# Grouping the half-height matmuls of a feed-forward block by four pairs, and spreading the side work of an attention loop over its tiles

## Chip, cores and metric

One core of a Trainium2 chip. The metric is the device time of one execution in microseconds (us), with the median of several executions as the time of a kernel. A profile is one execution of a kernel; its span is about 1.7 us shorter than the device time of the same execution.

## The reference

A transformer block whose LayerNorms are modulated by a vector `c`: linear attention with 32 heads of 18 channels, then a ReLU feed-forward part. All data are bfloat16; there are S = 2048 tokens, D = 576 and Dff = 4608.

```python
mod = (_silu(c) @ w_mod).reshape(1, 6, 1, -1)        # sa, ca, ga, sb, cb, gb
h = _layernorm(x) * (1 + ca) + sa
q, k, v = split(h @ wqkv)                            # 32 heads x 18
pq, pk = q @ w_phi, k @ w_phi                        # per head, 18 x 18
phi_q = concat([softmax(pq), softmax(-pq)])          # over the 18 channels
phi_k = concat([softmax(pk), softmax(-pk)])
kv, z = phi_k^T @ v, sum_s phi_k                     # no S x S matrix
o = (phi_q @ kv) / (phi_q @ z + 1e-6)
x = x + ga * (o @ wo)
h = _layernorm(x) * (1 + cb) + sb
x = x + gb * (relu(h @ w1) @ w2)
```

## The kernel before

The kernel first folds `w_phi` into the weights of k. A loop over 16 tiles of 128 tokens then does k, v, the softmax of k, and the accumulation of `kv` in PSUM. Other work is laid between the tiles: the fold of `w_phi` into the weights of q (five transposed weight blocks, then five fold steps), the transposed LayerNorm output ("features") for the next four tiles, the q projections, and rows and columns of the modulation. Then come two tiles of attention output, and the feed-forward part in five blocks of 2, 4, 4, 4 and 2 tiles, with the attention output of the next block's tiles inside.

Inside `manual_schedule` an engine's instructions keep the order of the program text. In the loop a scheduler orders them; `issue_after(x)` keeps an instruction behind `x`. `two()` gives one of two pairs of PSUM banks, `one()` a single bank.

```python
def k_tile(t):                                       # v_tile(t) is alike
    ps = two()
    project(lambda bk: ps[:, bk, :], lambda ci: hT[:, ci, t*P:(t+1)*P], wk_sb, HALF)   # 10 matmuls
    E = E_sb[:, t % NE]                              # NE = 3
    for sgn in range(2):
        nc.scalar.activation(out=E[:, sgn, :]..., in_=ps[:, :, 0:HD2], func=ACT.Exp, scale=1.0 - 2.0*sgn)

def k_softmax(t):
    nc.vector.tensor_reduce(out=R[:, 0, :], in_=E, axis=AXX, op=ALU.add)
    ...                                              # reciprocal
    for sgn, eng in ((1, nc.gpsimd), (0, nc.vector)):
        eng.tensor_tensor(out=e, in0=e, in1=..., op=ALU.mult)

def kv_tile(t):
    for g, (h0, nh) in enumerate(GRP):               # 5 groups of heads
        for sgn in range(2):
            nc.tensor.matmul(kvacc[g // 2][...], lhsT=E_sb[:, t % NE, sgn, ...], rhs=v_sb[:, t % NV, g, ...], ...)

for t in range(NT + 1):
    if t < NT:
        k_tile(t)
        v_tile(t)
        u = t + 4
        if u < NT:
            with tc.issue_after(held):               # held: LayerNorm of tile 3, so long past
                ln_stats(0, u)
            if u % 2:
                ln_rstd(0, u - 1, u + 1); ln_apply(0, u - 1); ln_apply(0, u)
            if u % 4 == 3:
                to_features(u - 3, 4, one, hT, (u - 3)*P, mod1, "aavva", 0)
    if 1 <= t <= NT:
        k_softmax(t - 1)
    if 2 <= t <= NT:
        kv_tile(t - 2)
    if t < NT:
        if t + 4 < NT and t % 4 == 3:
            for n in (1, 2):
                to_features(t + 1, 4, one, hT, (t + 1)*P, mod1, "aavva", n)
        a_filler(t)       # t=0: all wq transposes; t=1: whole wq fold; t=3: row; t=6: columns; q parts
```

```python
# feed-forward, hidden layer of one block: 18 pairs of hidden tiles
for j in range(NJ // 2):
    pace(9 * nn / 2400)                              # may put attention work here
    hps = [psf(), psf()]
    for half in (0, 1) if j % 2 == 0 else (1, 0):    # so two pairs share one trip to half height
        for n, jj in enumerate((j, j + NJ // 2)):
            # half 0: 4 matmuls over 128 rows; half 1: one matmul over 64 rows, pair members
            # on rows 0-63 and 64-127
            ...
    ...                                              # ReLU
```

The softmax here doesn't subtract the row's maximum and nothing guards it: scores larger than these inputs give would overflow.

## Time and profile before

The kernel before takes 461.5 us (median of four first executions).

| stretch of the profile | us |
|---|---|
| start to the first k tile | 18.5 |
| first k tile to the end of the last kv tile | 92.3 |
| from there to the first feed-forward matmul | 19.8 |
| feed-forward part | 327.7 |

The end of the last kv tile is counted here and below to the start of its last matmul. A granted clock of 0.50 is called half clock. In the views, `two` and `one` are the PSUM banks of the loop, `kvacc` the sums of `kv` in PSUM and `kvzd` their copies, `psf`, `num` and `pt` the PSUM banks of the feed-forward part, `rEQ` the exponentials of q; `rW`, `rV` and `rH` are regions of SBUF that hold weights, v, and the features, exponentials of k and hidden layer.

The stretches follow one another on TensorE, so that what one loses or gains moves all later ones.

### The profile page before, as it was taken

To read this page: it belongs to the slowest core of one execution; us is meant where nothing else is said; L and a number is where in the kernel's file an instruction comes from. 1 tells how busy PE (TensorE), PEld (TensorE's weight loads), DVE (VectorE), ACT (ScalarE), POOL (GpSimd) and SP (SyncE) were. 2 spreads that over 40 slices of the span, in tenths; PEclk is the share of its full clock that TensorE was granted. 3 is DMA by queue.
4 is the path that set the end of the run, shared out by engine and by line. 5 is a ranking of instruction groups with operands and counts; after the bars stand their busy time and mean duration, and the time that the engine had idled before them with its cause. 6 is when DMAs were issued, how large, how long until landed. Compare 5 with 4: busy or idle time off the path is not lost.

```text
span 458.2 us, 8190 instructions
## 1 busy us (share of the span) xinstructions
PE 433.4 (95%) x3448; PEld 297.0 (65%) x3460; DVE 237.5 (52%) x566; ACT 158.6 (35%) x387; POOL 57.8 (13%) x71
## 2 busy tenths in 40 slices
PE   5978999997889999999999999999999999999996
PEld 4756776775567785335888633488863348887775
DVE  4697864564844664334566433555743331564421
ACT  3656676765666412332111232212122230012300
POOL 8022141432111110001111000111100000110000
PEclk9698999999999999999999999999999999999999
DMA  7970750000076000000000000000000000000000
GB/s 230 346 215 0 276 191 2 1 0 3 0 256 210 1 14 14 1 0 1 14 14 14 14 0 1 1 2 26 14 13 1 0 1 13 15 14 14 1 0 28
DMA packets 17151, 22.52 MB, mean 49 GB/s; under 512 B 2010, under 2 KB 16474, under 8 KB 16602
## 3 DMA queue, kind: packets, MB, share of 16 engines
q1 hardware_dynamic: 15904, 21.97, 14.4%
q8 instruction: 27, 0.44, 0.4%
q10 hardware_dynamic: 1210, 0.02, 0.2%
q14 instruction: 10, 0.08, 0.1%
HBM read 19.63 MB, written 2.36 MB: 48 GB/s over the span
## 4 chain that ended last, share of the span: by engine, by line
PE 83%; ACT 6%; DVE 5%; POOL 4%; issue 1%; POOLq 0%; DVEq 0%; ACTq 0%
PE psf L657 31%; PE psf L638 28%; PE two L313 5%; PE psf L643 5%; PE psf L313 4%; PE two L380 2%; POOL rH L346 2%; ACT rH L324 2%; DVE R_sb L338 2%; PE num L518 2%; ACT rEQ L388 1%; PE kvacc L355 1%; POOL rW L164 1%; PE psf L293 1%; PE pt L574 1%
## 5 line engine op out<-in xcount | busy, mean ns | idle before, releaser
L638 PE MATMUL psf<-h2T,rW 128*128 128x512 bf16 (+1 forms) x708 | 132.3, 336 | 1.8 <-issue 0.9
L657 PEld LDWEIGHTS <-rH 128*128 128x128 bf16 x1152 | 111.2, 98 | 27.4
L657 PE MATMUL psf<-rW,rH 128*128 128x288 bf16 x864 | 116.3, 286 | 0.0
L638 PEld LDWEIGHTS <-rW 128*128 128x128 bf16 x720 | 66.5, 98 | 62.2 <-issue 15.3
L647 ACT ACTIVATE rH<-psf 128x256 bf16<-128x256 f32 (+1 forms) x108 | 51.8, 490 | 105.1 <-PE psf L643 84.8
L649 DVE TENSOR_SCALAR rH<-psf 128x512 bf16<-128x512 f32 (+1 forms) x72 | 45.0, 625 | 79.0 <-PE psf L643 39.7
L563 POOL TENSOR_TENSOR o_sb<-rV 128x576 bf16<-128x576 f32 x15 | 21.1, 1408 | 271.7 <-DVE rV L559 271.7
L313 PE MATMUL two<-rW,rH 128*128 128x288 bf16 (+2 forms) x320 | 46.6, 295 | 2.1 <-ACT rH L301 0.8
L657 PE MATMUL psf<-rEQ,rH 128*128 128x288 bf16 x288 | 41.3, 286 | 0.0
L313 PEld LDWEIGHTS <-rH 128*128 128x128 bf16 x320 | 31.5, 101 | 12.4 <-ACT rH L301 1.6
L660 DVE TENSOR_TENSOR yt<-psf,gb_row 128x288 f32<-128x288 f32 x32 | 14.4, 449 | 42.6 <-PE psf L657 42.6
L346 POOL TENSOR_TENSOR rH<-rH,R_sb 128x576 bf16<-128x576 bf16 x16 | 25.7, 1608 | 69.0 <-DVE R_sb L343 28.7
L338 DVE TENSOR_REDUCE R_sb<-rH 128x64 f32<-128x1152 bf16 x16 | 21.6, 1351 | 21.4 <-ACT rH L324 21.3
L272 ACT ACTIVATE rs<-mv,eps_t 128x1 f32<-128x1 f32 (+2 forms) x24 | 7.2, 298 | 58.6 <-DVE mv L269 56.1
L268 DVE BATCH_NORM_STATS2 st<-x_sb 128x6 f32<-128x288 bf16 x60 | 24.7, 439 | 2.0 <-DMA x_sb<-in_A_x_dram 1.6
L643 PE MATMUL psf<-h2T,rW 64*128 64x512 bf16 (+1 forms) x180 | 23.8, 339 | 0.0
L324 ACT ACTIVATE rH<-two 128x576 bf16<-128x576 f32 x32 | 19.3, 663 | 9.0 <-PE two L313 8.0
L546 DVE TENSOR_TENSOR ab<-dz 128x70 f32<-128x70 f32 x16 | 3.7, 232 | 35.4 <-ACT dz L537 35.4
L388 ACT ACTIVATE rEQ<-two 126x512 bf16<-126x512 f32 (+1 forms) x32 | 16.6, 601 | 10.5 <-PE two L380 10.5
L579 ACT ACTIVATE oT<-pt 128x640 bf16<-128x640 bf16 x14 | 9.9, 707 | 29.6 <-PE pt L574 29.6
L313 PE MATMUL psf<-wo_sb,oT 128*128 128x288 bf16 x140 | 19.4, 286 | 0.0
L380 PE MATMUL two<-rH 128*126 128x512 bf16 (+1 forms) x80 | 18.8, 380 | 0.4
(118 smaller groups left out, 389.9 us busy)
## 6 DMA issues: line engine op xcount, KB each, us to landing
rW<-in_B_w_dram SPq DMA_DIRECT2D x1, 4608.0 KB
rW<-in_B_w_dram SPq DMA_DIRECT2D x3, 1296.0 KB, 9.8
rW<-in_w_mod_dram SPq DMA_DIRECT2D x6, 576.0 KB, 7.4
out_dram<-x_sb SPq DMA_DIRECT2D x16, 144.0 KB, 1.8
rEQ<-in_B_w_dram SPq DMA_DIRECT2D x1, 1296.0 KB, 7.4
rW<-in_A_wqkv_dram SPq DMA_DIRECT2D x2, 576.0 KB, 8.8
x_sb<-in_A_x_dram SPq DMA_DIRECT2D x1, 1152.0 KB, 11.8
rW<-in_A_wqkv_dram SPq DMA_DIRECT2D x4, 144.0 KB, 3.1
```

What stands on the lines that cost most here:

```text
L268: nc.vector.bn_stats(out=s[:, hf, :], in_=x_sb[:, t, hf * HD2:(hf + 1) * HD2])
L313: nc.tensor.matmul(ps(bk)[:, 0:cn], lhsT=lhs(ci), rhs=rhs[:, ci, c0:c0 + cn], start=(first and ci == 0), stop=(ci == NC - 1))
L324: nc.scalar.activation(out=E[:, sgn, :].rearrange("p (b f) -> p b f", b=2), in_=ps[:, :, 0:HD2], func=ACT.Exp, scale=1.0 - 2.0 * sgn)
L338: nc.vector.tensor_reduce(out=R[:, 0, :], in_=E, axis=AXX, op=ALU.add)
L346: eng.tensor_tensor(out=e, in0=e, in1=R[:, 1, sgn * H:(sgn + 1) * H].unsqueeze(2).to_broadcast([P, H, DH]), op=ALU.mult)
L380: nc.tensor.matmul(pss[k][0:nf, :], lhsT=wq_sb[:, ci, f0:f0 + nf], rhs=hT[:, ci, sl], start=(ci == 0), stop=(ci == NC - 1))
L388: nc.scalar.activation(out=Eq[b][0:nf, g, sgn, :], in_=pss[k][0:nf, :], func=ACT.Exp, scale=1.0 - 2.0 * sgn)
L638: nc.tensor.matmul(hps[n][:, 0:nn], lhsT=w1a[:, ci, jj * P:(jj + 1) * P], rhs=h2T[:, ci, 0:nn], start=(not last and ci == 0), stop=(last a ...
L643: nc.tensor.matmul(hps[n][:, 0:nn], lhsT=w1b[b0:b0 + 64, j * P:(j + 1) * P], rhs=h2T[b0:b0 + 64, 4, 0:nn], start=not last, stop=last)
L647: nc.scalar.activation(out=H1[:, jj, 0:nn], in_=hps[n][:, 0:nn], func=ACT.Relu)
L649: nc.vector.tensor_relu(H1[:, jj, 0:nn], hps[n][:, 0:nn])
L657: nc.tensor.matmul(ps[:, 0:cn], lhsT=H1[:, j, tt * P:(tt + 1) * P], rhs=w2q[j // 9][:, j % 9, c0:c0 + cn], start=(j == 0), stop=(j == NJ - 1))
```

## The change

The intent is to keep TensorE busy. In the feed-forward part a group is four pairs instead of two, so that fewer trips into half height and back are needed; the PSUM pools of this part then hold 4 + 3 + 1 banks, and four pairs use all of them. In the loop, `kv_tile` runs three tiles behind k instead of two, the side work is spread over the tiles, and it stands ahead of `kv_tile`. At the end of attention, 24 dummy matmuls stand where TensorE waits. The core of the diff (cut: declarations, PSUM handles as lists of single banks, dummy allocations):

```diff
-    NE = 3
+    NE = 4                                   # and NV = 4
     def kv_tile(t):
-        for g, (h0, nh) in enumerate(GRP):
+        for g in (4, 0, 1, 2, 3):            # kv_final in the same order
...
-    def a_filler(t):
+    def filler_1(t):
         if t == 0:
-            fold_transposes(wq_raw, wqT, "av")
+            wq_transposes((0, 1), q_two)     # copies out of PSUM all on ScalarE
+        if t == 1:
+            wq_transposes((4,), lambda n: [one()])
+    def filler_2(t):
+        if t in (3, 7, 11):
+            next_features(t, 2)
+        if t == 0:
+            wq_transposes((2, 3), q_two)
-        if t == 1:
-            fold(wqT, wq_sb, "av")
+        if t in (2, 3):
+            fold(wqT, wq_sb, "av", (2 * t - 4, 2 * t - 3))
-        if t == 3:
-            mod_row(2, ga_row, one)
+        if t == 4:
+            fold(wqT, wq_sb, "a", (4,))
+            row_e(row_mm(2, q_two), ga_row)
...
+    LN_AT = {0: (4, 5), 1: (6, 7)}           # LayerNorm two tiles earlier
+    for t in range(2, NT - 6):
+        LN_AT[t] = (t + 6,)
+    LAG = 3
-    for t in range(NT + 1):
+    for t in range(NT + 2):
         if t < NT:
             k_tile(t)
+            filler_1(t)
             v_tile(t)
-            ...                              # LayerNorm, first part of the features
+        for u in LN_AT.get(t, ()):
+            later(ln_stats, 0, u)            # later: issue_after(held)
+            ...
         if 1 <= t <= NT:
-            k_softmax(t - 1)
+            held = k_softmax(t - 1)          # its reduction
-        if 2 <= t <= NT:
-            kv_tile(t - 2)
         if t < NT:
-            if t + 4 < NT and t % 4 == 3:
-                for n in (1, 2):
-                    to_features(t + 1, 4, one, hT, (t + 1) * P, mod1, "aavva", n)
-            a_filler(t)
+            filler_2(t)
+        if LAG <= t < NT + LAG - 1:
+            kv_tile(t - LAG)
+        if t < 12 and t % 4 in (1, 2):
+            next_features(t, t % 4 - 1)
...
+        size = 2 if b == 0 else 4
+        for j0 in range(0, NJ // 2, size):
+            js = list(range(j0, min(j0 + size, NJ // 2)))
+            for j in first half of js:   full(j, hp[j], False)
+            for j in js:                 rest(j, hp[j], ...)      # the half-height matmuls
+            for j in second half of js:  full(j, hp[j], True); relu(j, hp[j])
...
-    rps = row_mm(5, lambda: num3()[:, 0, :])
+    rps = row_mm(5, q_n3)
+    for _ in range(24):
+        nc.tensor.matmul(spare[0][:, 0:P], lhsT=ident[:, :], rhs=ident[:, :], start=True, stop=True)
```

(The three lines `for j in ...` of the feed-forward part are shortened here.)

## The prediction

> **What bounds the kernel now.** I read the page first (engine shares, then the 40 slices), then cut the span into five stretches with the windows view, then the list of waits of TensorE, then the timeline around the idle places. The slices say where to look:
>
> ```profile
> PE 433.4 (95%) x3448; PEld 297.0 (65%) x3460; DVE 237.5 (52%) x566; ACT 158.6 (35%) x387; POOL 57.8 (13%) x71
> ...
> PE   5978999997889999999999999999999999999996
> ...
> PEclk9698999999999999999999999999999999999999
> ```
>
> TensorE is the bound. It is full from about 130 us to the end (the feed-forward part) and has holes before (the attention part); PEclk is the granted clock. The windows view with the program's own borders (start, first k tile, first q part, last kv tile, first feed-forward matmul, end) sizes this; columns are the stretch, its length, then busy us (instructions) of PE, PEld, DVE, ACT, POOL, then clock and DMA:
>
> ```profile
> 19.77:50.05 30.28, 25.12 (x254) 18.95 (x253) 26.63 (x69) 18.69 (x53) 5.92 (x4) 0.94 0.42 125
> 50.05:110.22 60.17, 56.42 (x471) 41.79 (x471) 35.79 (x47) 40.70 (x86) 19.80 (x12) 1.00 0.23 87
> 110.22:130.45 20.23, 14.87 (x114) 10.25 (x114) 14.32 (x45) 11.55 (x33) 1.40 (x1) 0.92 0.06 11
> 130.45:458.17 327.72, 322.75 (x2450) 213.42 (x2461) 150.16 (x372) 78.89 (x200) 19.72 (x14) 1.00 0.07 24
> ```
>
> So TensorE idles 5.2 us in the second stretch, where VectorE is 88% busy, 3.7 us in the third, 5.4 us in the fourth, and hardly at all in the feed-forward part. Who it waits for (us in total, times, longest), and the two places where a wait is followed by a slow clock (timeline; start, duration, group, idle before it; and two windows):
>
> ```profile
> PE kvacc L355 <- POOL rH L346: 3.3, 5, 0.8
> PE n L518 <- DVE kvzd L367: 1.8, 1, 1.8
> PE two L257 <- ACT rV L333: 1.1, 1, 1.1
> PE kvacc L355 <- DVE rH L346: 0.9, 2, 0.5
> ```
>
> ```profile
> 33.48 6.73 PE L313 MATMUL two<-rW,rH 128*128 128x288 bf16 x40
> ...
> 112.70 2.31 PE L518 MATMUL n<-kvzd,rEQ 126*128 126x140 bf16 x20 [1.80 <-DVE kvzd L367]
> 114.81 5.22 PE L380 MATMUL s<-rH 128*126 128x512 bf16 x20
> ```
>
> ```profile
> 30.42:33.83 3.41, 1.78 (x19) 1.26 (x18) 3.29 (x10) 1.57 (x5) 1.74 (x1) 1.00 0.07 21
> 33.83:37.24 3.41, 3.41 (x17) 2.23 (x15) 1.64 (x6) 1.38 (x3) 0.00 (x0) 0.50 0.00 0
> 108.92:112.34 3.42, 1.16 (x11) 0.70 (x10) 1.92 (x10) 2.07 (x4) 1.25 (x1) 1.00 0.01 2
> 112.34:115.75 3.41, 3.05 (x23) 2.66 (x24) 1.42 (x8) 0.81 (x6) 0.00 (x0) 0.50 0.00 0
> ```
>
> Two stretches of 3.41 us in which TensorE is busy half the time or less are each followed by 3.41 us at half clock. The last view is the feed-forward inner loop: 16 full-height matmuls, then 4 of half height (64 rows, the last 64 of the 576 inputs):
>
> ```profile
> 182.97 0.61 PE L643 MATMUL psf<-h2T,rW 64*128 64x512 bf16 x4
> 183.51 3.63 PE L638 MATMUL psf<-h2T,rW 128*128 128x512 bf16 x16
> 187.07 0.60 PE L643 MATMUL psf<-h2T,rW 64*128 64x512 bf16 x4
> ```
>
> **What the Trainium skill says.** (1) "TensorE: Matmul & The Clock Gate", Part 1 (The HAM clock gate): the clock halves after about one idle window of 3.4 us and comes back after a busy one. The trace agrees on the length (3.41 us) and shows that half-idle is enough: the two windows above are 52% and 34% busy; one of 60% busy at 40.7 us did not trip it. (2) Same page, Part 3 (Packing small matmuls — row/col tiling): matmuls on different row groups run concurrently. The trace agrees: the four half-height matmuls take 0.54 us from first start to the next full one, not four times 0.216. (3) "TensorEngine Tiling (Array Packing)", Tiling Modes, Key Properties: "Mode switching requires drain". The trace agrees: one round is 187.07 - 182.97 = 4.10 us, while 16 full matmuls and 2 pairs at the streaming interval of 0.216 us (16 in 3.63 us, less the modelled 0.38 of the last, over 15 steps) would be 3.89. So one trip into half height and back costs 0.21 us. Single records say the same: 312 ns from the last full start to the first half-height start, 308 ns back, 229 ns from pair to pair; the weight load of 93 ns, hidden elsewhere, stands open at each switch. At 256 columns the excess is the same 0.21 us.
>
> **The change, part by part.** The order of instructions of both kernels, without times, is used below.
>
> *Feed-forward.* Blocks 1 to 4 go over hidden tiles by four pairs instead of two: 2 full pairs, 8 half-height matmuls, 2 full pairs. 18 pairs then need 5 trips instead of 9. A trip saved gives 0.20 us, less the 0.013 us that a further pair-to-pair step costs: 0.184 us. 4 trips x 4 blocks x 0.184 = 2.9 us. Block 0 keeps trips of two pairs, but two of its trips were cut in half by attention work placed inside (205 + 211 ns at such a cut instead of none): the new placement puts that work between, about 0.2 us each. Sum: **3.3 us**, all on the bound engine. The price is PSUM: four pairs hold all 8 banks, so the attention tile and its transposes share banks with the hidden tiles. By the order, in blocks 1 to 3 only one attention tile (before pair 16) falls into this phase, and its first six matmuls need banks whose ReLU (0.6 us) follows a matmul group that ended 1.7 us earlier; the third needs one that ended 0.86 us earlier. I count no wait. The added ScalarE copy per tile (0.2 us x 16) lies on an engine that is 24% busy there.
>
> *End of attention.* Before, the first numerator matmul waits for the whole row of 10 VectorE instructions (110.64 to 112.70). After, group 4 goes first and each piece is waited for by itself, so tile 0's matmuls overlap that row and end about 0.8 us earlier (113.2 instead of 113.95). From there to the first feed-forward matmul a VectorE chain leads (two tiles' divisions, LayerNorm, transposes: 114.4 to 130.45), with no change in length. So I count **0.9 us**. Fewer idle us there should also spare the half clock at 112.3, but that lies mostly beside the VectorE chain. The 24 dummy matmuls (1.3 us) fit where TensorE idled from 127.9 to 129.1 waiting for ScalarE and VectorE: no cost, no gain, except as a guard for the clock.
>
> *Attention loop.* The kv product lags by 3 tiles instead of 2 (fourth buffers of E and v), so it no longer waits for GpSimd's 1.7 us multiplication (3.3 us) or VectorE's (0.9 us). LayerNorm of later tiles is held behind the softmax reduction; before, VectorE did it for all 12 tiles by 50 us, ahead of what TensorE waited for. The fold of the q weights is spread over tiles 2 to 4, features over three tiles (the waits for them, 1.4 us, go). I walked through the new order with the old durations. One new wait: the transposes of wq now take the second pair of PSUM banks ahead of v tile 0, which then waits for ScalarE's three copies (3 x 0.55) and two exponentials (2 x 0.55): TensorE is done with k at 21.8 and starts v at 23.8, so 2.0 us are lost. Afterwards the walk finds waits of 0.2 to 0.5 us only: k2 at 29.6, k3 at 33.9, k4 at 38.9, q part 0 at 43.7, against 50.05 before. At that point the new order has 10 kv matmuls (0.7 us) and 41 column matmuls (1.2 us) fewer behind it, so the real lead is 4.4 us: 1.7 of it from the half clock at 33.8 not occurring, the rest from waits. From there to k tile 15 (102.9 before) the rest of the 3.7 us of idle time and some switching shrink; the walk gives 7.1 us of lead in all. A walk by hand misses small waits; I take **6 us**. The lead holds to the last kv tile: the chain k15, softmax, multiplication (6.0 us) is as long as before, and the kv work put off is done inside it.
>
> Sum: 461.5 - 3.3 - 0.9 - 6.0 = 451.3 us.
>
> **Rivals.** *A: the early ScalarE wait takes back the loop's gain.* For it: ScalarE gets all five wq copies (0.65 each, two were VectorE's) exactly when k0's exponentials are due, and the 2.0 us of idle time in one window is near what tripped the clock. If it does, another 1.7 us go, and later tiles start late: gain in the loop 2 to 3 us, total about 455. Against: VectorE, 88% busy there, was the tighter engine. *B: the feed-forward blocks wait on PSUM.* With all banks in use each group could wait for the ReLU of the last (0.6 us, 4 groups x 3 blocks = 7 us): gain undone, total near 458. Against: the banks needed next were freed a full 3.4 us before. *C: the loop is bound by TensorE's streaming after all and the walk is right in full:* idle time almost gone, clock never halved, total 449. For it: streaming work between 20 and 110 us is only 72 us of 90 (columns over the interval of 288 columns in 0.123 us).
>
> **Range and chances.** The feed-forward term is firm to 0.5 us, the end of attention to 0.7, the loop runs from 2 to 8. That gives 448.5 to 455.5. The 2% line is at 452.3, one us above my value, so faster by over 2% gets 0.61, within 2% 0.37, slower 0.02 (B with A).
>
> **What would show it.** Right: a round of four pairs takes 8.0 us (32 + 4 intervals of 0.216 plus 0.24); the feed-forward stretch falls from 327.7 to about 324.4; waits for GpSimd's L346 under 1 us; no half clock at 30 to 40 or at 112; a wait of about 2 us for ScalarE before v tile 0; first feed-forward matmul at about 123.5. Wrong: waits on ScalarE or VectorE between half-height matmuls (B), a half clock before 35 us (A), or a first feed-forward matmul later than 128.

## The result

The changed kernel takes 445.34 us (median of nine executions, 444.89 to 447.78), against 460.72 us of the kernel before in the same rounds (median of twelve). The ratio is 0.9676, with a 95% interval of 0.9659 to 0.9694: faster by 3.2%, and outside the predicted range at its low end. Ratios here and below are the mean time of one kernel's runs over that of the other's of the same rounds, so not quite the ratio of the quoted medians.

The first profile of the changed kernel fell on the slowest of its nine executions. Its slices of TensorE and of the granted clock show why (span 446.06 us):

```profile
PE   5898999998799999999999999999999999999996
PEclk8589999999999999999999999999999999999999
```

The half clock from about 9 us lasted 17.07 us. A second run of the same kernel (a_again, below) gave a profile with 10.24 us there, as the kernel before had, so that one is compared. The two profiles differ at the beginning alone: the second k tile starts at 26.84 us and at 23.94, which is the whole 2.9 us between their spans. Engine shares, slices and clock of that run:

```profile
PE 425.2 (96%) x3472; PEld 298.1 (67%) x3484; DVE 237.4 (54%) x564; ACT 159.0 (36%) x405; POOL 54.5 (12%) x71
...
PE   5999999997899999999999999999999999999996
...
PEclk9699999999999999999999999999999999999999
```

TensorE is 8.2 us less busy although it has 24 more instructions; 3.5 of that is in the feed-forward part (322.75 to 319.27 in the windows view). Of its holes only the one at the tenth and eleventh slices is left, the end of attention. The windows view, with the same borders by program place as in the prediction (stretch, length, busy us of PE, PEld, DVE, ACT and POOL, clock, DMA share, GB/s):

```profile
18.64:42.40 23.76, 22.06 (x213) 17.50 (x214) 22.32 (x50) 19.43 (x52) 4.79 (x5) 0.98 0.54 171
42.40:99.61 57.21, 55.92 (x520) 42.73 (x518) 42.37 (x67) 40.20 (x86) 17.52 (x12) 1.00 0.26 94
99.61:118.87 19.26, 14.99 (x140) 10.40 (x139) 14.24 (x45) 12.85 (x36) 1.53 (x2) 1.00 0.10 24
118.87:443.16 324.29, 319.27 (x2450) 216.09 (x2461) 148.85 (x372) 78.80 (x214) 19.72 (x14) 1.00 0.07 23
```

In the second row (first q part to last kv tile) TensorE now idles 1.3 us (57.21 - 55.92), 3.75 before. Two of its waits (total us, times, longest):

```profile
PE n L550 <- ACT rEQ L385: 1.4, 1, 1.4
...
PE psf L308 <- ACT rH L676: 0.4, 1, 0.4
```

The waits for GpSimd's and VectorE's multiplication ahead of the kv product (3.3 and 0.9 us before) are not in the list any more. The first line is a new wait at the end of attention, for ScalarE's exponentials; the second is the one new wait inside the feed-forward part.

Where the time went, from the profile before (span 458.17) to that of a_again (443.16):

| term | before | after | gain | predicted |
|---|---|---|---|---|
| end of the last kv tile (from the start) | 110.70 | 100.28 | 10.4 | 6.0 |
| from there to the first feed-forward matmul | 19.75 | 18.59 | 1.2 | 0.9 |
| feed-forward part | 327.72 | 324.29 | 3.4 | 3.3 |

The sum is 15.0 us. Two of the three terms are near their numbers; the loop is not.

### The profile page after: what moved, and what is told of

It reads as the page before. It is cut to its first block, busy times and chain, and to the rows that moved or that the text cites.

```text
span 446.1 us, 8251 instructions
## 1 busy us (share of the span) xinstructions
PE 427.2 (96%) x3472; PEld 299.2 (67%) x3484; DVE 237.2 (53%) x564; ACT 159.0 (36%) x405; POOL 54.5 (12%) x71
## 4 chain that ended last, share of the span: by engine, by line
PE 85%; ACT 5%; DVE 3%; DMA 3%; issue 1%; SPq 1%; DVEq 0%; ACTq 0%
PE psf L713 32%; PE psf L666 17%; PE num L666 8%; PE two L308 6%; PE two L377 4%; PE psf L308 4%; ACT rEQ L385 3%; DMA rW<-in_A_wqkv_dram 3%; PE psf L672 3%; PE pt L666 3%; PE num L550 2%; PE num L672 1%; PE kvacc L352 1%; PE psf L288 1%; PE pt L607 1%
## 5 line engine op out<-in xcount | busy, mean ns | idle before, releaser
L713 PEld LDWEIGHTS <-rH 128*128 128x128 bf16 x1152 | 111.2, 98 | 27.4
L666 PEld LDWEIGHTS <-rW 128*128 128x128 bf16 x720 | 68.0, 98 | 58.7 <-issue 9.3
L666 PE MATMUL psf<-h2T,rW 128*128 128x512 bf16 (+1 forms) x458 | 81.9, 327 | 0.6 <-ACT h2T L758 0.3
L676 ACT ACTIVATE rH<-psf 128x512 bf16<-128x512 f32 (+1 forms) x58 | 26.9, 492 | 80.4 <-PE psf L672 76.7
L680 DVE TENSOR_SCALAR rH<-psf 128x512 bf16<-128x512 f32 (+1 forms) x40 | 23.5, 619 | 47.2 <-PE psf L672 44.4
L308 PE MATMUL two<-rW,rH 128*128 128x288 bf16 (+2 forms) x320 | 45.5, 295 | 1.8 <-ACT rEQ L385 1.0
L308 PEld LDWEIGHTS <-rH 128*128 128x128 bf16 x320 | 31.6, 101 | 11.0 <-issue 2.2
L666 PE MATMUL num<-h2T,rW 128*128 128x512 bf16 (+1 forms) x186 | 38.3, 352 | 0.6 <-issue 0.5
L718 DVE TENSOR_TENSOR rYT<-psf,gb_row 128x288 f32<-128x288 f32 x32 | 14.4, 450 | 43.5 <-PE psf L713 43.4
L341 POOL TENSOR_TENSOR rH<-rH,R_sb 128x576 bf16<-128x576 bf16 x16 | 22.4, 1403 | 64.8 <-DVE R_sb L338 22.6
L676 ACT ACTIVATE rH<-num 128x512 bf16<-128x512 f32 (+1 forms) x32 | 17.4, 544 | 22.8 <-PE num L666 22.8
L308 PE MATMUL psf<-wo_sb,oT 128*128 128x288 bf16 x140 | 19.4, 286 | 0.4 <-ACT rH L676 0.4
```

What stands on the lines that cost most here:

```text
L308: nc.tensor.matmul(ps(bk)[:, 0:cn], lhsT=lhs(ci), rhs=rhs[:, ci, c0:c0 + cn], start=(first and ci == 0), stop=(ci == NC - 1))
L341: eng.tensor_tensor(out=e, in0=e, in1=R[:, 1, sgn * H:(sgn + 1) * H].unsqueeze(2).to_broadcast([P, H, DH]), op=ALU.mult)
L666: nc.tensor.matmul(ps[:, 0:nn], lhsT=w1a[:, ci, jj * P:(jj + 1) * P], rhs=h2T[:, ci, 0:nn], start=(not last and ci == 0), stop=(last and c ...
L676: nc.scalar.activation(out=H1[:, j, 0:nn], in_=hps[0][:, 0:nn], func=ACT.Relu)
L680: nc.vector.tensor_relu(H1[:, j + NJ // 2, 0:nn], hps[1][:, 0:nn])
L713: nc.tensor.matmul(ps[:, 0:cn], lhsT=H1[:, j, tt * P:(tt + 1) * P], rhs=w2q[j // 9][:, j % 9, c0:c0 + cn], start=(j == 0), stop=(j == NJ - 1))
```

## Experiments

Each kernel was timed in rounds beside the kernel before, which had medians of 460.85, 460.86, 460.85, 461.1 and 460.93 us in the five sessions (in this order: a_again to a_ln_free; a_fold_old to b_guard; a_feat_burst to a_kv_order; l_feat to c_pool; c_pool_dma and c_dma). Each session ran on another chip. "Undone" is said of a part of the change put back in the changed kernel; times are medians with their range.

### The changed kernel again (a_again)

No edit.

> The changed kernel once more, to have a second profile of it, because the first one fell on the slowest of nine runs (447.8 us, with 17 us of half clock at the start against 10 in the profile of before). My theory: the usual run has the half clock for 7 to 10 us at the start and at no other place before the end, takes 445.3 us and reaches the first q part near 43 us, 2 us earlier than the first profile (45.3). Rival: the usual run is like the profile, q part 0 at 45 us, and the 2.5 us are elsewhere (in the feed-forward part, or before the first k tile).

Measured: 444.98 us (444.46 to 447.15), ratio 0.9669; the first q part starts at 42.4 us, and between 19.5 us and the end the profile has no half clock, as the theory had it. Over both sets of executions the time goes with the mean granted clock: those at 0.985 or more took 444.5 to 445.7, those at 0.98 took 447.1 to 447.8. Single experiments can therefore shift by some 2 us from chance at the start, and a difference of about 1 us between medians is weak evidence, the more where ranges overlap.

### Feed-forward trips back to two pairs (a_trips2)

```diff
-        size = 2 if b == 0 else 4
+        size = 2
```

> The changed kernel with the feed-forward loop in groups of two pairs in all blocks (9 trips into half height per block in place of 5). Theory, from 0.184 us a trip: 16 trips more, +2.9 us, so 448.2 us; a round of two pairs 4.10 us. Rival (sharing all 8 banks costs waits that the profile hides): less than +2 us or none. Rival (the trip costs more than the interval shows, because weight loads behind it are late too): over +4 us.

Measured: 448.36 us (448.05 to 448.75), 3.4 more than a_again; feed-forward stretch 327.64 us. So sixteen saved trips are worth 3.38 us, 0.21 each; the prediction had 0.184. A round of the changed kernel in the timeline of a_again shows it (start, duration, engine, group):

```profile
176.94 0.61 PE L672 MATMUL psf<-h2T,rW 64*128 64x512 bf16 x4
177.38 0.59 PE L672 MATMUL num<-h2T,rW 64*128 64x512 bf16 x3
177.60 0.38 PE L672 MATMUL pt<-h2T,rW 64*128 64x512 bf16 x1
177.91 2.76 PE L666 MATMUL num<-h2T,rW 128*128 128x512 bf16 x12
180.51 1.03 PE L666 MATMUL pt<-h2T,rW 128*128 128x512 bf16 x4
181.37 3.62 PE L666 MATMUL psf<-h2T,rW 128*128 128x512 bf16 x16
184.92 0.61 PE L672 MATMUL psf<-h2T,rW 64*128 64x512 bf16 x4
```

From 176.94 to 184.92 are 7.98 us for four pairs (8.0 predicted), and no group waits for a bank: there is no bracket with an idle time. Eight half-height matmuls take 0.66 us from the first start to the last, so pairs after the first cost the streaming interval alone.

### Lag of two tiles again (a_lag2), LayerNorm not held (a_ln_free)

```diff
-    LAG = 3
+    LAG = 2
```

> The changed kernel with the kv product two tiles behind again in place of three, four buffers kept. If the lag is what took the waits for GpSimd and VectorE away (4.2 us of idle time in the kernel before): +3 to +4 us, about 449 us, with 'kvacc waits for rH' back in the list of TensorE's waits. If the LayerNorm work held behind the softmax is what brought the softmax forward in time, the third tile of lag is worth under 1 us.

Measured: 446.28 us (445.69 to 448.65), 1.3 more than a_again, with overlapping ranges. End of the last kv tile 101.58 us (100.28 in a_again); the list of waits has 0.5 us for GpSimd's multiplication. The lag, to which the prediction gave the 4.2 us of waits for GpSimd and VectorE, is worth about a third of that here.

For a_ln_free the LayerNorms of the loop are held behind that of tile 3, as before, and not behind the newest softmax reduction:

```diff
+    held_ln = held                           # taken before the loop, not updated
...
-            later(ln_stats, 0, u)
+            later_ln(ln_stats, 0, u)         # also ln_rstd, ln_apply
```

> The changed kernel with the LayerNorm of later tiles no longer held behind the newest softmax reduction (held only behind the first four tiles, as before). If VectorE's order was the cause of the slow early part: +2 to +4 us, with the first q part later than 45 us. If the lag of three tiles covers it anyhow: within 0.7 us of the changed kernel.

Measured: 445.14 us (444.6 to 445.42), ratio 0.9663 beside 0.9669: no effect that these rounds can see.

### Fold, features and the whole loop as before (a_fold_old, a_feat_old, a_loop_old)

a_fold_old does all wq transposes at tile 0 and the whole fold at tile 1:

```diff
     def filler_1(t):
-        ...
+        pass
     def filler_2(t):
         if t == 0:
-            wq_transposes((2, 3), q_two)
+            fold_transposes(wq_raw, wqT, "av")
         if t == 1:
+            fold(wqT, wq_sb, "av")
...
-        if t in (2, 3):
-            fold(wqT, wq_sb, "av", (2 * t - 4, 2 * t - 3))
```

> The changed kernel with the q-weight fold as before: all 25 transposes at tile 0, all five fold steps at tile 1. Theory: the lead is made here, because in the trace k tile 2 starts at 27.4 us in place of 33.5, and the old burst of fold steps waits for its own evictions: +4 to +6 us (about 450), with k tile 2 after 31 us, and a half clock after it in some runs. Rival (the burst is only work moved, the lead comes from lag, holding and features): under +1.5 us.

Measured: 446.04 us (446.0 to 450.53; four of six within 0.1 of 446.0), 1.1 more than a_again; last kv tile ends at 101.43 us. K tile 2 does start late, at 32.2 us (27.4 in a_again), but k tile 4 at 38.0 (37.4): the burst mostly moves work, as the rival said.

a_feat_old puts all three parts of the features at every fourth tile, and with that also puts `kv_tile` ahead of the fillers:

```diff
-        if t in (3, 7, 11):                  # in filler_2
-            next_features(t, 2)
...
+        if t < 12 and t % 4 == 3:
+            next_features(t, 0)
         if 1 <= t <= NT:
             held = k_softmax(t - 1)
-        if t < NT:
-            filler_2(t)
         if LAG <= t < NT + LAG - 1:
             kv_tile(t - LAG)
-        if t < 12 and t % 4 in (1, 2):
-            next_features(t, t % 4 - 1)
+        if t < 12 and t % 4 == 3:
+            next_features(t, 1); next_features(t, 2)
+        if t < NT:
+            filler_2(t)
```

> The changed kernel with the features of the next four tiles made in one burst at every fourth tile, as before. Theory: TensorE waited 1.4 us for these evictions before (0.8 for ScalarE, 0.6 for VectorE), three bursts: +1 to +2 us. Rival (LayerNorm is now two tiles earlier, so the burst is harmless): under +0.7 us.

Measured: 449.46 us (448.57 to 450.29), 4.5 more. It is the largest single part, but the edit undoes two things; a_feat_burst and a_kv_first below separate them.

a_loop_old puts the whole old loop with its fillers into the changed kernel (kv group order, feed-forward part and end stay changed).

> The changed kernel with the whole attention loop as before (lag 2, fold, features, LayerNorm, q bias row), the rest as changed. If the parts add up: +10.4 us, the lead at the end of the last kv tile in the second profile, so about 455.4, and 3.4 + 1.1 us faster than the kernel before (456.3). If the parts depend on each other (a shorter end shifts no clock, the feed-forward part hides some): 453 or less, or 457 or more.

Measured: 455.68 us (455.36 to 456.44), 10.7 more than a_again. The last kv tile ends at 109.95 us, 9.7 later. The other 0.8 us stand behind the loop: the profile has half clocks of 3.41 us again, at 33.27 and at 111.78 us, and from the last kv tile to the first feed-forward matmul it takes 19.39 us instead of 18.59, with the new end in both. So the terms of the loop and of the end are not independent: with the old loop the half clock behind it is back. Its list of waits has those for the multiplication back:

```profile
PE kvacc L352 <- POOL rH L341: 3.1, 6, 0.8
...
PE kvacc L352 <- DVE rH L341: 0.9, 2, 0.5
```

### The kernel before without its half clocks (b_guard)

Dummy matmuls in the kernel before, at the two places where it waits long:

```diff
-            fold(wqT, wq_sb, "av")
+            fold(wqT, wq_sb, "av", guard=8)  # 8 matmuls of 128 columns after each fold step
...
     kv_tile(NT - 1)
+    gd = one()
+    for _ in range(28):
+        nc.tensor.matmul(gd[:, 0:P], lhsT=ident[:, :], rhs=ident[:, :], start=True, stop=True)
```

> The kernel before, with dummy matmuls that write PSUM columns nobody reads: 8 behind each fold step of the q weights and 28 behind the last kv tile, where TensorE waits anyway; so no window of 3.4 us should be idle enough to halve the clock. If a half clock of 3.41 us costs the 1.7 us that it takes from dense work: the one at 33.8 us gives 1.7, the one at 112 some 0.3 (beside the VectorE chain): 458.5 to 459 against 460.8. Rival (TensorE waits for the other engines there anyway, so its clock is worth nothing): within 0.5 us of the kernel before or slower by the dummies.

Measured: 458.22 us (457.92 to 458.82), ratio 0.9944 (0.993 to 0.9958): 2.6 us less than before, for the two stretches at half clock together. The window ahead of the first former half clock, and that window itself:

```profile
30.42:33.83 3.41, 3.37 (x61) 3.16 (x59) 3.41 (x10) 1.74 (x7) 1.16 (x1) 1.00 0.09 27
33.83:37.24 3.41, 3.03 (x26) 2.17 (x25) 3.41 (x14) 2.04 (x7) 0.00 (x0) 1.00 0.00 0
```

TensorE was 52% busy in the first window before and was halved in the second; here it is 99% busy, and the clock stays at 1.00. (The record of the clock in this profile begins at 21.16 us and has no half clock until the end.) The 2.6 us are a net value, for the dummies take TensorE time too: k tile 2 starts at 34.43 us, 33.48 before. In the profiles, 1.3 us of it can be placed: k tile 15 starts 0.5 earlier, and from the last kv tile to the first feed-forward matmul it takes 18.95 us instead of 19.75; the rest can be chance at the start. That the remainder of the loop's gain is waiting and order is a conclusion by exclusion.

### Features in a burst, kv ahead of the fillers (a_feat_burst, a_kv_first)

```diff
-        if t in (3, 7, 11):                  # a_feat_burst, in filler_2
-            next_features(t, 2)
...
+        if t < 12 and t % 4 == 3:            # kv_tile stays behind the fillers
+            for n in range(3):
+                next_features(t, n)
...
-        if t < 12 and t % 4 in (1, 2):
-            next_features(t, t % 4 - 1)
```

> The changed kernel with the features in one burst at every fourth tile, but with the q parts ahead of the kv product, as changed. (The run before it, which cost 4.4 us, undid both.) If the burst is the cause: +3 to +4 us, 448 to 449, with waits for the feature evictions. If the order of kv and q parts was: under +1.5 us.

Measured: 449.48 us (448.6 to 450.7), 4.5 more than a_again. The burst alone accounts for a_feat_old. In its timeline the second burst, ahead of k tile 8, looks like this (in brackets the idle time and who ended it):

```profile
58.46 0.41 PE L308 MATMUL two<-rW,rH 128*128 128x288 bf16 x2
59.36 0.30 PE L308 MATMUL two<-rW,rH 128*128 128x288 bf16 x1 [0.49 <-DVE rH L299]
59.49 0.20 PE L352 MATMUL kvacc<-rV,rH 128*72 128x73 bf16 x1
59.81 0.40 PE L288 MATMUL one<-ident,xn 128*128 128x128 bf16 x4
...
60.17 0.51 PE L352 MATMUL kvacc<-rV,rH 128*72 128x73 bf16 x6
```

The next k tile (L308) can only start where a part of the features is written, so it goes by one and two matmuls, between transposes (L288) and kv products (L352) that are short and wait for other engines. The kernel before has the same shape at its first burst:

```profile
42.22 0.56 PE L355 MATMUL kvacc<-rV,rH 128*126 128x127 bf16 x6 [0.75 <-POOL rH L346]
42.62 0.39 PE L313 MATMUL two<-rW,rH 128*128 128x288 bf16 x2
...
42.97 0.61 PE L293 MATMUL one<-ident,xn 128*128 128x128 bf16 x8
43.42 0.39 PE L313 MATMUL two<-rW,rH 128*128 128x288 bf16 x2
44.22 0.40 PE L313 MATMUL two<-rW,rH 128*128 128x288 bf16 x2 [0.41 <-DVE rH L304]
```

In a_again k and v of the same tile run as one row of twenty:

```profile
57.97 2.61 PE L308 MATMUL two<-rW,rH 128*128 128x288 bf16 x20
```

In the list of waits of a_feat_burst the one for GpSimd comes back although the lag is three, with 1.5 us; the waits that name features have 0.7. The loss of 4.5 is larger than both. Tile by tile, k tile 5 starts at 45.0 us (44.5 in a_again), k tile 9 at 66.4 (64.7) and k tile 13 at 88.1 (84.3): the kernel is 0.5 us late after the first burst, 1.7 after the second and 3.8 after the third.

```diff
-        if t < NT:
-            filler_2(t)                      # a_kv_first
         if LAG <= t < NT + LAG - 1:
             kv_tile(t - LAG)
+        if t < NT:
+            filler_2(t)
```

> The changed kernel with the kv product ahead of the fillers (q parts, fold), as before, and the features spread as changed. If kv standing behind a q part is what hides the softmax chain and the GpSimd multiplication: +2 to +4 us, with waits of kvacc for GpSimd. If the lag of three tiles hides it alone: under +0.7 us.

Measured: 446.5 us (444.98 to 447.79), 1.5 more in the median, but four of its six executions had a granted clock of only 0.98 (its profile has 17.07 us of half clock at the start), and the ranges overlap. Its best executions (445.0 and 445.4) are at most 0.5 us slower than those of a_again, so this order is worth little.

### Without the dummies, and kv groups in natural order (a_no_dummy, a_kv_order)

```diff
-    for _ in range(24):
+    for _ in range(0):
```

> The changed kernel without its 24 dummy matmuls ahead of the feed-forward part. Theory: from 115.6 to 118.9 us TensorE would be busy about 1.3 us of 3.3, so in many runs the first feed-forward matmuls run 3.4 us at half clock, and there TensorE is the bound: +1.0 to +1.7 us in those runs. Rival (the prediction: a mere guard): within 0.3 us in all runs, slower clock nowhere.

Measured: 445.89 us (444.66 to 446.96). Three of six executions are as fast as a_again (444.7 to 445.4), three are slower (446.4 to 447.0). The profile fell on a slow one:

```profile
115.78:119.20 3.42, 1.73 (x21) 1.32 (x19) 2.01 (x9) 2.58 (x9) 0.00 (x0) 1.00 0.45 96
119.21:122.62 3.41, 3.08 (x16) 1.68 (x16) 2.64 (x9) 1.29 (x7) 0.00 (x0) 0.50 1.09 392
```

A window in which TensorE is 51% busy is followed by 3.41 us at half clock, now at the beginning of the feed-forward part, where TensorE sets the time; that part takes 325.68 us. In the profiles with the dummies there is no half clock at this place, and no cost of them is seen (the fastest execution here takes 444.66 us, with them 444.46).

```diff
-        for g in (4, 0, 1, 2, 3):            # kv_tile and kv_final
+        for g in range(NG):
```

> The changed kernel with the groups of the kv product and of its final pass in the natural order 0 to 4. The prediction counted 0.8 to 0.9 us for the early start of the first numerator tile. But in the trace that tile waits 1.4 us for ScalarE's exponentials of q part 9, not for VectorE's kvzd. If it is the exponentials that set its start: within 0.4 us. If the order is worth its 0.8 us: 445.8.

Measured: 446.71 us (445.45 to 447.43), 1.7 more in the median, with overlapping ranges. Its list of waits has the old one back, and the profile has a half clock of 3.41 us behind it, at 102.79 us:

```profile
PE n L550 <- DVE kvzd L364: 1.9, 1, 1.9
```

The prediction gave this order 0.8 or 0.9 us. From the last kv tile to the first feed-forward matmul this profile takes 20.03 us, 0.6 more than that of a_loop_old, which has the half clock too, and 1.4 more than that of a_again, which has none. So by these profiles the order is worth 0.6 us, and 0.8 more where it prevents the half clock; that it does not come in every execution is read from the mean clocks alone (one of the six, at 445.45 us, has 0.988).

### Single parts in the old loop (l_feat, l_lag, l_feat_lag)

As parts that are undone one by one do not add up (1.3 + 1.1 + 4.5 + 0.2 is 7.1, not 10.7), parts were also added to a_loop_old alone: the features spread, with the LayerNorm two tiles earlier that this needs (l_feat), the lag (l_lag), both (l_feat_lag).

```diff
-            u = t + 4                        # l_feat
+            for u in {0: (4, 5), 1: (6, 7)}.get(t, (t + 6,) if t < NT - 6 else ()):
...
-            if t + 4 < NT and t % 4 == 3:
-                for n in (1, 2):
-                    to_features(t + 1, 4, ...)
+            if t < 12 and t % 4:
+                t0 = t // 4 * 4 + 4
+                to_features(t0, 4, one, hT, t0 * P, mod1, "aavva", t % 4 - 1)
-    for t in range(NT + 1):                  # l_lag
+    for t in range(NT + 2):
-        if 2 <= t <= NT:
-            kv_tile(t - 2)
+        if 3 <= t <= NT + 1:
+            kv_tile(t - 3)
```

> The changed kernel with the old attention loop (455.7 us), to which alone the spread features and the LayerNorm two tiles ahead are added. If the features are worth what undoing them costs: -4.5 us, 451.2. If they only help once the kv product lags and the fold is spread: 454 or more.

> The changed kernel with the old attention loop (455.7 us), to which alone the lag of three tiles is added. If the waits for GpSimd and VectorE (3.1 + 0.9 us in its list) are worth their sum: 452. If only what undoing the lag costs: 454.4. If the waits only move to other places of the old order: 455 or more.

> The changed kernel with the old attention loop (455.7 us) and both the spread features and the lag of three tiles. If the parts add: the sum of the two gains before it, near 450. If they hold each other up, less than the better of the two alone plus 0.5 us.

| kernel | us (range) | less than a_loop_old (455.68) |
|---|---|---|
| l_feat | 450.18 (448.46 to 451.38) | 5.5 |
| l_lag | 453.12 (452.34 to 454.31) | 2.6 |
| l_feat_lag | 449.7 (448.34 to 450.01) | 6.0 |
| a_again | 444.98 | 10.7 |

(a_loop_old and a_again are from other sessions; the kernel before differed by 0.3 us at most between them.) Spread features with the earlier LayerNorm give more than half of the loop's gain. The lag alone gives 2.6; once the features are spread, the 0.5 that it adds lies inside the ranges. The gains do not add (5.5 and 2.6 would be 8.1). The lists of waits show a part of the reason. With the lag of two and spread features (l_feat), all the waits of the kv product are:

```profile
PE kvacc L352 <- POOL rH L341: 0.8, 1, 0.8
```

With the lag of three and bursts (l_lag) they are:

```profile
PE kvacc L352 <- POOL rH L341: 2.2, 3, 0.8
...
PE kvacc L352 <- DVE rH L341: 0.9, 2, 0.5
```

So of the waits for the multiplication (3.1 and 0.9 us in a_loop_old) spreading the features takes 3.2 of the 4.0 away, a third tile of lag only 0.9. But the lists do not account for the times: all of TensorE's waits in the loop and just behind it sum to 8.2 us in a_loop_old and 6.7 in l_feat, which has new ones, while k tile 15 starts 5.7 us earlier.

Nor is it the same gain at the same place as in a_feat_burst. In l_feat 4.6 us of it are there by k tile 5 and 5.8 by k tile 13; in a_feat_burst 0.5 and 3.8 are lost by these tiles. One reason may be the clock: a_loop_old has half clocks at 33.27 and 111.78 us, l_feat only one at 106.09, l_lag only one at 33.44 and l_feat_lag only one at 31.33. So the 5.5 us of l_feat include whatever the half clock cost that it lacks at 33 us; that was not split off.

The remaining 4.7 us, from l_feat_lag to a_again, come with the fold spread over tiles, the fillers ahead of kv, the held LayerNorm, the row on a pair of banks and the half clock at 31.33, together. They were not split further.

### Attempts at a still faster version (c_pool, c_pool_dma, c_dma)

Before the loop, TensorE waits 3.1 us for GpSimd. c_pool moves GpSimd's fills that are needed later behind the building of the block-diagonal `w_phi`; c_dma loads the weights of q ahead of those of v; c_pool_dma does both.

```diff
-    for z in zeros:                          # c_pool
-        nc.gpsimd.memset(z, 0.0)
-    ...                                      # ones of v, pieces of kvzd
+    nc.gpsimd.memset(zeros[0], 0.0)
     build_bdw()
+    rest_of_pool()
-    load_rows(nc.sync, wv_sb, A_wqkv[:, 2 * D:3 * D])      # c_dma
-    nc.sync.dma_start(x_sb[:, 4:8, :], xf[:, 4:8, :])
     load_rows(nc.sync, wq_raw, A_wqkv[:, 0:D])
+    nc.sync.dma_start(x_sb[:, 4:8, :], xf[:, 4:8, :])
+    load_rows(nc.sync, wv_sb, A_wqkv[:, 2 * D:3 * D])
```

> The changed kernel with GpSimd building the block-diagonal fold weights ahead of its other memsets and copies, so that the first fold of the k weights need not wait from 7 to 10 us. If that chain sets the first k tile: -1 to -1.5 us, 443.7. If the loads do (the first k tile stands behind transposes of wq, which land at 18.5 us): within 0.4 us of 445.

Measured: 446.22 us (445.94 to 448.36), not faster. The first k tile starts at 18.87 us, no earlier than in a_again. The wait is replaced by one for the weights of q:

```profile
PE one L436 <- DMA rW<-in_A_wqkv_dram: 2.1, 1, 2.1
```

> GpSimd builds the fold weights first, and wq is loaded ahead of x tiles 4 to 7 and of wv. If wq's load was the last thing that held the first k tile: it starts near 17.3 us in place of 18.6, and the kernel takes 443.7 to 444.2 against 445.0. If the later x tiles and wv then hold tile 4's LayerNorm or v tile 0: within 0.5 us of 445.

> The changed kernel with the order of loads alone changed. wq is then there in time but the k fold is still late: the first k tile as before (18.5 us), the kernel within 0.4 us of 445. If it gains over 0.6 us, wq's load alone set the first k tile.

Measured: c_pool_dma 445.23 us (443.71 to 445.9), ratio 0.9652 (0.9618 to 0.9685); c_dma 445.16 us (444.81 to 445.25), ratio 0.9658. Neither is clearly better than the changed kernel (0.9669, 0.9641 to 0.9697). In the profile of c_pool_dma the first k tile does start earlier, at 17.27 us instead of 18.64, but the half clock at the start lasts 13.65 us instead of 10.24, and the second k tile starts at 24.9 us instead of 23.9. In that of c_dma it starts at 18.40 us, as expected. Whether moving GpSimd's fills causes the longer half clock, or that was chance, is open; all six executions of c_pool have a mean clock of 0.985 or less, as three of six of c_pool_dma and two of six of a_again.

## Why the prediction was wrong

**The feed-forward term was right** (3.4 for 3.3), though its parts were off against each other: the trip is worth 0.21 us where 0.184 was counted (the prediction had measured 0.21 itself, then took 0.20, less 0.013 for a further half-height pair, which is 0.187), since such a pair costs next to nothing beyond its streaming, and block 0 gave about 0.1 where 0.4 was counted; a new wait there of 0.4 us for a ReLU (L676) fits the difference. That wait is for a PSUM bank; between the groups of four pairs, where rival B had put them, there are none.

**The end of attention came near its number (1.2 for 0.9), in part by luck.** Counted was a start of the numerators 0.8 us earlier, and next to nothing for the half clock at 112.3, "mostly beside the VectorE chain". The first numerator now waits 1.4 us for ScalarE's exponentials, which the prediction had not seen, and starts 1.65 us after the last kv matmul, 2.00 before. Without the half clock the old end takes 0.8 less (18.95 us in b_guard for 19.75), and with it the new end takes 0.8 more (19.39 in a_loop_old for 18.59). So 0.8 of the 1.2 us is the half clock that no longer occurs, and 0.4 the new end. The dummies show no cost and guard, as was said.

**The loop term failed: 6.0 predicted, 10.4 measured.** The walk through the order can be held against the tiles of a_again:

| start of | walk | measured |
|---|---|---|
| k tile 2 | 29.6 | 27.4 |
| k tile 3 | 33.9 | 31.9 |
| k tile 4 | 38.9 | 37.4 |
| q part 0 | 43.7 | 42.4 |
| k tile 15 | 95.8 | 93.0 |

Three steps failed, and all made the gain too small.

1. "One new wait ... 2.0 us are lost" did not occur. The 2 us are missing from k tile 2 on. The step had v tile 0 wait for the copies of the transposes and for the exponentials of k tile 0, so as if it got the pair of banks of k tile 0. The timeline of a_again:

```profile
20.50 0.22 PE L435 MATMUL one<-ident,rW 64*72 64x64 bf16 x1
20.64 2.30 PE L308 MATMUL two<-rW,rH 128*128 128x288 bf16 x17
23.16 0.62 PE L432 MATMUL two<-ident,rW 128*126 128x128 bf16 x8 [0.22 <-ACT rH L319]
```

The row of 17 is the rest of k tile 0 and all of v tile 0, without a gap; v begins at 21.56 us, before ScalarE has begun with k's exponentials (21.92). So v got the pair of the first wq transposes. ScalarE's copies of that pair (start, duration) ended at 21.5 us, just in time:

```profile
20.31 1.19 ACT L438 ACTIVATE rW<-two 126x576 bf16<-126x576 bf16 x2 [0.74 <-PE two L435]
```

It was the next transposes (the third line of TensorE) that got k's pair, and waited 0.22 us. For the feed-forward part the prediction read the banks from the order of instructions; for this step it shows no such reading. Rival A, built on the same wait, falls with it.

2. "The walk gives 7.1 us of lead in all ... I take 6" took 1.1 us off in the wrong direction. The walk had already counted a wait that did not exist. Rival C, the walk in full, pointed the right way, and even it was too slow. (Its 449 is not the walk's sum, which is 461.5 - 3.3 - 0.9 - 7.1 = 450.2; and the ranges of the three terms, added up, give 448.1 to 456.5 and not 448.5 to 455.5.)

3. "Features over three tiles (the waits for them, 1.4 us, go)" was mis-sized: the part is worth 4.5 us where undone and 5.5 alone in the old loop (there with a half clock less). The working counted only the waits that name the features, and put the 4.2 us of waits for the multiplication down to the lag. The experiments turn that round: with the features spread and the old lag, 0.8 us of these waits are left. The burst also cuts k tiles into pieces, and the tiles after it start later. How it makes the kv products wait for GpSimd (they may stand in line too early) is argued, not tested. The lag, taken for 4.2 us, is worth 1.3 where undone and 2.6 alone.

The same shows in the second half of the walk, from q part 0 to k tile 15, which was another 1.5 us too slow. The prediction let the idle time "and some switching" shrink there. In the windows view TensorE's idle time falls by 2.4 us (3.75 to 1.3), but its busy time falls too, by 0.5, although 49 more matmuls lie in this stretch (the prediction priced those at 1.9). By this estimate another 2.4 us of what was recorded as busy before were no work but matmuls that came one by one; that part was mis-sized.

Summed up: the predicted 6.0, the discount of 1.1, the 2.8 by which the walk was late at k tile 15 (1.3 until q part 0, where the false wait of 2.0 had partly been made up by small waits that the walk missed, and 1.5 after), and 0.5 between k tile 15 and the last kv tile make 10.4.

Of the signs that the prediction named, these were as told: the round of four pairs (7.98), the feed-forward stretch (324.3), GpSimd's waits under 1 us, no half clock at 30 to 40 or at 112. Two were not: the wait before v tile 0, and the first feed-forward matmul, at 118.9 us and not at about 123.5.

What stays open: how the last 4.7 us of the loop split among the fold, the order of the fillers, the held LayerNorm, the row and the half clock at 31 us; undone singly, the fold costs 1.1 us, the order of the fillers 0.5 at most in its best executions and the held LayerNorm 0.2; the row was not undone.

## What to carry to other kernels

A wait in the list names who came last, not the part that made the queue: size a burst of side work by when the next main tiles start with and without it, not by the waits that bear its name. Before counting a wait on a rotating buffer, read from the order of instructions which buffer each user takes. Where several parts remove the same wait, undo each and also add each alone, as the two answers differ. Before comparing two profiles, list their stretches at half clock: a part can gain by its work, or by keeping one window busy enough.

## What the Trainium skill lacked or had wrong

- "TensorE: Matmul & The Clock Gate", Part 1 (The HAM clock gate) says that the clock is halved after an idle window of about 3.4 us. The runs agree on the length and show that a partly idle window is enough: windows with TensorE 52%, 34% and 51% busy were each followed by 3.41 us at half clock. Near 60% it goes either way: one at 40.66 us of the kernel before was not followed by it, one of 60% at 27.92 us of l_feat_lag was. The page gives no such share. The half clock at the start of a kernel lasted 10.24, 13.65 or 17.07 us in different profiles, which are whole multiples of 3.41; executions of the changed kernel with the lower mean clock are the slow ones (447.1 to 447.8 us against 444.5 to 445.7).
- What the prediction took from the same part, that the clock comes back after a busy window, did not hold at the start: in a_kv_first TensorE is busy all through 15.02 to 18.44 us, with one-column matmuls and then transposes, and two more windows at half clock follow; in the kernel before, 112.34 to 115.75 us, 89% busy with matmuls of 140 and 512 columns, was enough. The kind of work may be the reason; no run tests it.
- "TensorEngine Tiling (Array Packing)", Tiling Modes, Key Properties says "Mode switching requires drain" and gives no cost. Here it is 0.21 us for a trip from 128 rows to 64 and back, at 256 as at 512 columns, and for eight half-height matmuls as for four (0.22 and 0.21).
- "TensorE: Matmul & The Clock Gate", Part 2, Back-to-back issue gap, gives about 131 ns for each matmul of 512 columns in a sustained stream and calls its formula (columns over 2.4, plus 2.5 ns) the isolated case. The stream here has 216 ns (16 in 3.62 us, less the modelled end of the last), which is the formula's value.
- The same page, Part 3, The mechanism, says that weight loads overlap matmuls in flight only where the row groups differ, though further up it also lets a load for the background weight buffer go ahead. Here the loads of full height, all on the same rows, are hidden (98 ns each, beside a matmul interval of 216), so the narrower sentence does not hold; at a change of height the interval is 312 - 216 = 96 ns longer, about one load (93 ns).
